# Five unread TensorE products in chunk 0's joins, and chunk 1's queries loaded ahead of weight piece 2

## The chip, the cores and the metric

The kernel runs on one core of one Trainium2 chip. The metric is the device time of one execution in microseconds (us). A profiled execution gives the trace, in which TensorE is PE, VectorE is DVE, ScalarE is ACT, GpSimd is POOL, and SyncE (SP) issues most of the DMA transfers.

## The reference

The kernel computes a DeltaNet attention block and then a SiLU feed-forward block on its output. Cut to what matters:

```python
# q, k, v: (4, 8, 768, 48); beta: (4, 8, 768)
k_n = k / (norm(k) + 1e-06)
state = zeros((B, H, D, D))
for t in range(S):
    y[:, :, t] = q[:, :, t] @ state
    v_old = k_n[:, :, t] @ state
    state += beta * outer(k_n[:, :, t], v[:, :, t] - v_old)
# bridge: (B, H, S, D) -> (B * S, H * D), 3072 tokens of 384
h = x @ w_in            # 384 x 2048
g = h * sigmoid(h)
return (g @ w_out)      # 2048 x 384
```

The weights arrive in 64-bit floating point, and the kernel turns them into 32 bits itself.

## The kernel before

The 768 steps of a sequence are cut into six chunks of 128, and a chunk into two halves of 64. Inside a chunk the recurrence is solved in matrix form: for each head a triangular matrix of 64 x 64 is inverted, and its blocks are put together on TensorE. Chunk 0 does this in its own way. `invert_first` inverts blocks of 16 x 16 on VectorE in 16 steps, and `joins` puts them together in ten stages for one half of the chunk: `corner`, `turned`, `straight` and `merge_half`, for the two groups of heads g = 0 and 1 in turn. Each stage is 32 or 64 small products on TensorE followed by copies out of PSUM by ScalarE and VectorE. The second merges (the last two stages) give the joined blocks `xi`. Then `solve(0)` starts: `inner` (tile pz, L859), whose results are copied out into `sums_of_w` (a slab) and `z`, then `first_outputs` (L905), which read the slab.

`joins(hf, between)` takes a list of things to do, one after each stage. `kept` is `busy(1)`: one product of 128 x 384 with the identity, into a PSUM bank of the CC pool, that nothing reads. `filled(n)` runs `fill` n times, `begin_next` starts the next piece of weights that has been asked for, `sized` scales chunk 0's values and does `begin_next`, and `none` does nothing. Ahead of `joins`, the 17 steps of the inverse have a list of words of their own; "n" there is one `busy(1)` too.

The weights are loaded in 16 pieces, `w_in` first. `fetch_w_in(i)` issues three transfers of 256 KB. `narrow` turns a piece into 32 bits in steps: two on ScalarE (L231, L232) when the piece is begun, one on VectorE (L236), and one on VectorE (L240) with an addition on GpSimd (L244) to end it. `fill` takes the steps in the order of the pieces.

Transfers go out on SyncE's queue in the order of the program, each tied to the one before. The list `pace` makes the next transfer wait for a given instruction, and `deep` makes each transfer wait until the one two places ahead of it has landed:

```python
        if pace or depth:
            behind(dma, pace.pop() if pace else line[-2], Sync)
```

`load_q(1)` issues the six transfers of chunk 1's queries into the room of `sums_of_g`; TensorE transposes them (L521) between the two halves of chunk 0's first outputs.

All instructions are pinned in the written order on their engines: `pin` ties each to the one before it on the same engine. After `joins(0, ...)` a text of one-letter words sets the order of the rest of the first stretch: "s" is a step of `solve`, "f" a `fill`, "T" and "q" transposes of chunk 1's keys and queries, "j" products of the second half's joins, "r" a step of the feed-forward block, "b" is `begin_next`.

Of the kernel before, what the change touches and what calls it, by code (L numbers as in the profile page):

```python
# [19 lines left out]
def kernel(  # L20
# [11 lines left out]
    B, H, S, D = q.shape  # L32
# [8 lines left out]
    T = 32  # L41
# [36 lines left out]
    pins = {}  # L78

    def pin(op):  # L80

        engine = op.ins.engine
        if engine in pins:
            behind(op, pins[engine])
        pins[engine] = op
        return op

    line, pace, depth = [], [], []
# [21 lines left out]
    def together(*parts):  # L110
        for _ in zip_longest(*parts):
            pass
# [58 lines left out]
    def linked(fetch, *args, of=None):  # L171

        pace.append(of or line[-1])
        fetch(*args)

    def deep(fetch, *args):

        depth.append(True)
        fetch(*args)
        depth.pop()  # L180
# [22 lines left out]
    seen_on = pin(nc.vector.memset(seen[:], 0.0)).ins.engine  # L203
# [9 lines left out]
    for e in range(2):  # L213
        for g in range(2):
            to, of = slice(HH * e + HH // 2 * g, HH * e + HH // 2 * (g + 1)), slice(HH // 2 * g, HH // 2 * (g + 1))
# [129 lines left out]
    def busy(n=1, after=None, how=NoSync):  # L345

        for _ in range(n):
            pw = bank(CC, "pw")
            done = pin(nc.tensor.matmul(  # L349
                pw[:, 0:DM], lhsT=ident[:],  # L350
                rhs=states[0][:].rearrange("p u a w -> p (u a w)")[:, 0:DM], start=True, stop=True,
            ))
            if after is not None:
                behind(done, after, how)
                after = None
# [158 lines left out]
    def turn(c, b, j, room, by_vector=False):  # L514

        if j == 0:
            kq_room(c, b)
        src, kq = (kbufs[c % 2], queries[c] if c < 2 else None)[j][:, b], kqs[c, b]
        pt = bank(room, "pt")
        for p in range(NP):  # L520
            pin(nc.tensor.transpose(  # L521
                pt[:, p * C : (p + 1) * C], src[:, p].rearrange("p e w -> p (e w)"), ident[:]
            ))
        ptv = pt[:].rearrange("p (a t) -> p a t", a=NP)
        if j == 1:
            if by_vector:
                pin(nc.vector.tensor_scalar(
                    out=kq[:, :, j, :], in0=ptv, scalar1=-1.0, scalar2=None, op0=ALU.mult
                ))
            else:  # L530
                pin(nc.scalar.mul(kq[:, :, j, :], ptv, -1.0))
        elif by_vector:
            pin(nc.vector.tensor_copy(out=kq[:, :, j, :], in_=ptv))
        else:
            pin(nc.scalar.copy(kq[:, :, j, :], ptv))

    def score(c, b, js, rooms, evacuate):

        g, u = b // HB, b % HB
        if (c, g) not in aps:  # L540
            aps[c, g] = {}
        for j in js:
            if j not in aps[c, g]:
                aps[c, g][j] = work.tile([P, HB, H, W], FP32, name=f"ap{j}", tag=f"ap{j}", bufs=2)
        ap, kq, n = aps[c, g], kqs[c, b], len(js)
        pa = [bank(room, f"pa{e}") for e, room in enumerate(rooms)]
        for p in range(NP):
            for e, hf in ((0, 0), (1, 1), (0, 1), (1, 0)):
                rows, half = slice(W * e, W * e + D), slice(W * hf, W * (hf + 1))
                pin(nc.tensor.matmul(  # L550
                    pa[e][half, p * n * W : (p + 1) * n * W], lhsT=kq[rows, p, 0, half],
                    rhs=kq[rows, p, js[0] : js[-1] + 1, half], start=True, stop=True,
                ))
        for e in range(2):
            of = pa[e][:, 0 : NP * n * W].rearrange("p (a j t) -> p a j t", a=NP, j=n)
            for i, j in enumerate(js):
                evacuate(j, e, ap[j][:, u, e::2, :], of[:, :, i, :])
# [6 lines left out]
    def by_act(to, of):  # L564
        return pin(nc.scalar.copy(to, of))  # L565
# [246 lines left out]
    def merge_half(g, hf, second):  # L812

        y = ys[0][:, g]
        pms = [bank(room, "px" if second else "py") for room in (A, CC)]
        for i in range(HH // 2):
            for e in range(2):
                n, k = 2 * i + e, hf ^ e ^ g
                even, odd = slice(W * k, W * k + T), slice(W * k + T, W * (k + 1))
                if second:  # L820
                    to, left, right = even, y[odd, n, :], xis[g][odd, n, T:W]
                else:
                    left = aps[0, g][0][even, n // H, n % H, T:W]
                    to, right = odd, xes[0][even, g * HH + n, :]
                yield pin(nc.tensor.matmul(
                    pms[k][to, T * i : T * (i + 1)], lhsT=left, rhs=right, start=True, stop=True
                ))
        for k, by in enumerate((by_act, by_dve)):
            e, half = hf ^ k ^ g, slice(W * k, W * k + T) if second else slice(W * k + T, W * (k + 1))
            of = pms[k][half, 0 : HH // 2 * T].rearrange("p (h t) -> p h t", t=T)  # L830
            by(xis[g][half, e::2, T:W] if second else y[half, e::2, :], of)
# [411 lines left out]
    class Piece:  # L1243
# [3 lines left out]
        def begin(self):  # L1247
            if self.steps is None:
                kind, i = self.name
                self.steps = (narrow_w_in if kind == "in" else narrow_w_out)(i)  # L1250
                next(self.steps)
# [73 lines left out]
    def first_score(b):  # L1325

        def evacuate(j, e, to, of):
            by_act(to, of)

        score(0, b, (0,), (A, CC), evacuate)  # L1330
# [49 lines left out]
    for n in range(1 + Q):  # L1380
        done = next(inv)
        for word in [
            "s2", "n s3", "u0", "u1 w0", "w1", "u2", "u3", "w2", "w3", "n", "N", "", "", "", "", "", "",
        ][n].split():
            at = int(word[1:] or 0)
            if word[0] == "b":
                busy(1, done, Sync)
            elif word[0] == "n":
                busy(1)
            elif word[0] == "s":  # L1390
                first_score(at)
            elif word[0] == "u":
                turn(0, at, 1, M)
            elif word[0] == "w":
                score(0, at, (1,), (A, CC), lambda j, e, to, of: by_act(to, of))
            else:
                begin(("in", 0))
# [6 lines left out]
    def joins(hf, between=()):  # L1404

        for stage in (
            corner(0, hf), corner(1, hf), turned(0, hf), turned(1, hf), straight(0, hf), merge_half(0, hf, False),
            straight(1, hf), merge_half(1, hf, False), merge_half(0, hf, True), merge_half(1, hf, True),
        ):
            yield from stage  # L1410
            for what in between[:1]:
                for one in what if isinstance(what, tuple) else (what,):
                    one()
            between = between[1:]
# [4 lines left out]
    def filled(n):  # L1419
        return lambda: fill(n)  # L1420

    def fetched():
        linked(fetch_w_in, 2, of=pins[seen_on])
        deep(load_q, 1)
        for i in (3, 4, 5, 6):
            deep(fetch_w_in, i)

    def sized():
# [3 lines left out]
    def none():  # L1432
        pass

    together(joins(0, [none, fetched, none, sized, filled(2), none, filled(1), none, begin_next, none]))

    pieces = chained(hidden(0, 0), hidden(0, 1), project())

# [132 lines left out]
                pieces = chained(feed_forward(1, 0), feed_forward(1, 1))  # L1571

    for text in (
        "s f s f T f q T s q T j5 j4 j8 j8 f j5 f q r T j20 j5 j8 j4 j16 j5 j4 b r q r f j4 j4 f W7 r b j4 f2 j4 j4 j32 r f e j6 j6 b j8 j4 f j4 j20 f j4 r j4 j99 l h f2 b l s w2 f r2 l p r s l w3 r p r l p f l2 f l3 b l f l2 s l f l p l3 r l3 s l f l r l2 p f s2 l2 H f l4 f r2 f p2 v l g G r i p i p r2 f i i2 r i r i b l i r f r i r b r2 i b b b i2 r2 i2 f b i5 r6 f r f r i2 r2 f r i r f r f i4 f i b r2 i3 b f b f r i r i f k r f r z i b r s r2 t z s b r2 b s m2 r5 t f t m f t m2 r s t m r b s b m r m2 s r m r m r c m2 s m r m t b m2 s m2 b m f m2 t r t m3 r m s m",
    ):
        script(text)
    for c in range(1, NCH):
# [59 lines left out]
```

## Time and profile before

| | |
|---|---|
| median of 3 runs | 641.72 us (639.18 to 643.24) |
| profiled execution | 639.7 us |
| its span, first to last instruction | 638.0 us |
| mean granted TensorE clock | 0.986 |
| TensorE busy | 621.5 us, 97% of the span |
| VectorE, ScalarE, GpSimd busy | 399.1, 216.7, 94.2 us |

The span is cut into 40 slices on the page, and a digit gives the busy share of a slice in tenths; the row PEclk gives the TensorE clock that was granted. Busy times of TensorE hold pipelined products, so that a busy TensorE can still run at half its clock. Times of instructions are given from the span's start.

### The profile page before, as it was taken

The page shows a single profiled execution, that of the slowest core. Times are in us where ns is not written, and L with a number is a line of the kernel's source. Part 1 is how long each engine was busy: PE and PEld are TensorE (multiplying, and loading weights), DVE is VectorE, ACT ScalarE, POOL GpSimd, SP SyncE. Part 2 cuts the span into 40 slices and gives each one's busy share as a digit, 9 for nine tenths or more (in the row PEclk, how much of TensorE's full clock was granted, in tenths as well). Part 3 has the DMA queues.
Part 4 walks back from the last instruction along what each step waited for, and adds up shares of the span by engine and source line. Part 5 has one row for each costly group of instructions (what it writes and reads, how often), then busy time and mean ns, then how long its engine had stood idle before and what let it go on. Part 6 is the DMA issues. An engine that isn't in the chain of part 4 may idle for free.

```text
span 638.0 us, 21886 instructions
## 1 busy us (share of the span) xinstructions
PE 621.5 (97%) x9650; PEld 547.8 (86%) x9650; DVE 399.1 (63%) x902; ACT 216.7 (34%) x510; POOL 94.2 (15%) x95
## 2 busy tenths in 40 slices
PE   8789999999999999999999999999999999999997
PEld 5678788666789989989989989989999989989997
DVE  6855879998765975654976564986564964212112
ACT  3565665152251122451122451122451122441110
POOL 5423531246010020020020010020001000000000
PEclk9968999999999999999999999999999999999999
DMA  7845554160459242369242259233173033100101
GB/s 152 182 124 179 179 128 100 52 149 3 102 120 163 57 89 24 83 126 147 39 107 29 69 122 160 56 88 37 43 142 72 19 83 34 39 15 1 26 0 26
DMA packets 141694, 53.68 MB, mean 84 GB/s; under 512 B 113296, under 2 KB 135056, under 8 KB 141600
## 3 DMA queue, kind: packets, MB, share of 16 engines
q1 hardware_dynamic: 141120, 51.62, 39.6%
q8 instruction: 76, 1.25, 0.9%
q10 hardware_dynamic: 480, 0.67, 0.3%
q14 instruction: 18, 0.15, 0.1%
HBM read 39.62 MB, written 10.49 MB: 79 GB/s over the span
## 4 chain that ended last, share of the span: by engine, by line
PE 95%; DVE 3%; issue 1%; POOL 0%; ACT 0%; DVEq 0%; POOLq 0%
PE phid L1068 40%; PE px L1175 17%; PE py L1175 13%; PE po L1103 7%; PE pa L550 3%; PE pz L859 2%; PE ph L847 2%; PE pyc L940 2%; PE pyc L927 2%; PE pu L879 2%; PE pt L521 1%; PE px L801 1%; PE py L801 1%; PE pw L349 1%; PE pl L752 1%
## 5 line engine op out<-in xcount | busy, mean ns | idle before, releaser
L1068 PE MATMUL phid<-xT,w_in 128*128 128x256 f32 x1152 | 258.7, 383 | 0.1
L1068 PEld LDWEIGHTS phid<-xT,w_in 128*128 128x128 f32 x1152 | 217.1, 191 | 30.6 <-issue 1.0
L1078 ACT ACTIVATE gT<-phid 128x512 f32<-128x512 f32 x88 | 52.6, 598 | 145.0 <-PE phid L1068 140.7
L648 DVE SCALAR_TENSOR_TENSOR rank<-g,step,x 128x31 f32<-128x31 f32 (+15 forms) x124 | 49.7, 401 | 35.8 <-DMA g<-blocks 32.4
L1157 DVE TENSOR_TENSOR sums_of_g<-gT 128x384 f32<-128x384 f32 (+1 forms) x60 | 29.7, 514 | 56.5 <-ACT gT L1078 45.9
L1175 PE MATMUL py<-w_out,sums_of_g 128*128 128x192 f32 x320 | 56.8, 329 | 0.0
L1175 PE MATMUL px<-sums_of_w,sums_of_g 128*128 128x192 f32 x320 | 56.6, 329 | 0.0
L1175 PEld LDWEIGHTS px<-sums_of_w,sums_of_g 128*128 128x128 f32 x320 | 52.2, 190 | 0.5
L1175 PEld LDWEIGHTS py<-w_out,sums_of_g 128*128 128x128 f32 x320 | 52.2, 190 | 0.4
L653 DVE TENSOR_TENSOR x<-x,rank 128x31 f32<-128x31 f32 (+15 forms) x124 | 42.5, 343 | 4.3
L488 POOL TENSOR_TENSOR vf<-vf,n_slot 128x768 f32<-128x768 f32 x10 | 15.2, 1538 | 168.4 <-DMA vf<-in_v_dram 168.4
L886 DVE TENSOR_TENSOR state<-state,pu 48x384 f32<-48x384 f32 x44 | 24.3, 552 | 23.2 <-PE pu L879 22.3
L565 ACT COPY xT<-pyc 48x128 f32<-48x128 f32 (+2 forms) x120 | 31.2, 260 | 1.6
L509 DVE STREAM_TRANSPOSE kq<-stage 128x512 f32<-128x512 f32 x28 | 28.3, 1114 | 3.6 <-DMA stage<-in_q_dram 3.5
L1175 PE MATMUL py<-w_out,gT 128*128 128x192 f32 x160 | 28.4, 329 | 0.0
L1175 PE MATMUL px<-sums_of_w,gT 128*128 128x192 f32 x160 | 28.4, 329 | 0.0
L1175 PE MATMUL px<-w_out,gT 128*128 128x192 f32 x160 | 28.0, 327 | 0.0
L859 PEld LDWEIGHTS pz<-vf,xi 64*64 64x64 f32 x768 | 25.1, 142 | 3.2 <-issue 2.2
L571 POOL COPY g<-x 64x256 f32<-64x256 f32 x4 | 5.0, 1247 | 152.3 <-DVE x L656 152.3
L1175 PEld LDWEIGHTS px<-w_out,gT 128*128 128x128 f32 x160 | 26.4, 190 | 0.5
L859 PE MATMUL pz<-vf,xi 64*64 64x48 f32 x768 | 26.8, 226 | 0.0
L1175 PEld LDWEIGHTS py<-w_out,gT 128*128 128x128 f32 x160 | 26.1, 190 | 0.3
(202 smaller groups left out, 827.7 us busy)
## 6 DMA issues: line engine op xcount, KB each, us to landing
vf<-in_v_dram SPq DMA_DIRECT2D x48, 96.0 KB, 2.7
out_dram<-o SPq DMA_DIRECT2D x42, 96.0 KB, 2.2
w_out<-in_moe_w_in_dram SPq DMA_DIRECT2D x12, 256.0 KB, 3.3
sums_of_w<-in_moe_w_out_dram SPq DMA_DIRECT2D x8, 384.0 KB, 3.7
blocks<-ap SPq DMA_DIRECT2D x40, 64.0 KB, 1.9
kb<-in_k_dram SPq DMA_DIRECT2D x12, 192.0 KB, 4.4
kb<-in_k_dram SPq DMA_DIRECT2D x24, 96.0 KB, 4.6
raw<-in_moe_w_in_dram SPq DMA_DIRECT2D x9, 256.0 KB, 3.5
```

The lines of the kernel that those rows point to most:

```text
L509: pin(nc.vector.transpose(out=kqs[c, b][:, :, j, :].rearrange("p a (i m) -> p a m i", i=T), in_=src.rearrange("p a (m d) -> p a m d", d=D) ...
L550: pin(nc.tensor.matmul(pa[e][half, p * n * W : (p + 1) * n * W], lhsT=kq[rows, p, 0, half], rhs=kq[rows, p, js[0] : js[-1] + 1, half], sta ...
L565: return pin(nc.scalar.copy(to, of))
L648: pin(nc.vector.scalar_tensor_tensor(out=tv, in0=g[:, 0:m, m : m + 1].to_broadcast([P, m, n]), scalar=step[:, m : m + 1], in1=x[:, m : m + ...
L653: yield pin(nc.vector.tensor_tensor(out=x[:, 0:m, m:T], in0=x[:, 0:m, m:T], in1=tv, op=ALU.add))
L859: yield pin(nc.tensor.matmul(pz[rows, n * D : (n + 1) * D], lhsT=xis[g][rows, u * H + 2 * p + e, :], rhs=vfs[c][rows, hf, g * HB + u, p, : ...
L886: pin(nc.vector.tensor_tensor(out=to, in0=to, in1=by_heads(pu[of]), op=ALU.add))
L1068: pin(nc.tensor.matmul(ph[:, j * GT : (j + 1) * GT], lhsT=w_in[:, a, (2 * f + j) * P : (2 * f + j + 1) * P], rhs=xTs[c, hf][:, a, :], star ...
L1078: pin(nc.scalar.activation(out=hidden_of(c, hf, f), in_=ph[:], func=ACTF.Silu, scale=-0.5 if in_blocks(c) else 0.5))
L1103: pin(nc.tensor.matmul(pos[i][:, 0:DM], lhsT=hidden_of(0, hf, f // 2)[:, at : at + C], rhs=w_outs[f // HFF][:, f % HFF, :], start=(f == 0) ...
L1157: pin(nc.vector.tensor_tensor(out=sums_of_g[:, k, fs], in0=of[0], in1=of[1], op=op))
L1175: pin(nc.tensor.matmul(to, lhsT=at, rhs=quarter(f, *b) if isinstance(b, tuple) else sums_of_w[b][:, f], start=start and f == 0, stop=f == ...
```

## The change

One more "n" stands in the words of the inverse's steps. In the list of `joins(0, ...)` four of the entries become `kept`, one of them beside `fetched`. The filling step that ended piece 0 moves from the seventh place to the tenth, and `begin_next`, which begins piece 2, moves from the ninth place out of the list to the head of the text as the word "b". In `fetched` the queries of chunk 1 go ahead of weight piece 2: they now wait for VectorE's instruction, and piece 2 is issued `deep`, as pieces 3 to 6 are.

```diff
-            "s2", "n s3", "u0", "u1 w0", "w1", "u2", "u3", "w2", "w3", "n", "N", "", "", "", "", "", "",
+            "s2", "n s3", "u0", "u1 w0", "w1", "u2", "u3", "w2", "w3", "n", "N", "", "n", "", "", "", "",
...
     def fetched():
-        linked(fetch_w_in, 2, of=pins[seen_on])
+        pace.append(pins[seen_on])
         deep(load_q, 1)
-        for i in (3, 4, 5, 6):
+        for i in (2, 3, 4, 5, 6):
             deep(fetch_w_in, i)
...
-    together(joins(0, [none, fetched, none, sized, filled(2), none, filled(1), none, begin_next, none]))
+    together(joins(0, [none, (fetched, kept), kept, sized, filled(2), kept, none, none, kept, filled(1)]))
...
-        "s f s f T f q T s q T j5 j4 j8 j8 f j5 f q r T ...
+        "b s f s f T f q T s q T j5 j4 j8 j8 f j5 f q r T ...
```

More of the change, by code (lines that the diff above doesn't have):

```diff
@@ L1573 @@
     for text in (
-        "s f s f T f q T s q T j5 j4 j8 j8 f j5 f q r T j20 j5 j8 j4 j16 j5 j4 b r q r f j4 j4 f W7 r b j4 f2 j4 j4 j32 r f e j6 j6 b j8 j4 f j4 j20 f j4 r j4 j99 l h f2 b l s w2 f r2 l p r s l w3 r p r l p f l2 f l3 b l f l2 s l f l p l3 r l3 s l f l r l2 p f s2 l2 H f l4 f r2 f p2 v l g G r i p i p r2 f i i2 r i r i b l i r f r i r b r2 i b b b i2 r2 i2 f b i5 r6 f r f r i2 r2 f r i r f r f i4 f i b r2 i3 b f b f r i r i f k r f r z i b r s r2 t z s b r2 b s m2 r5 t f t m f t m2 r s t m r b s b m r m2 s r m r m r c m2 s m r m t b m2 s m2 b m f m2 t r t m3 r m s m",
+        "b s f s f T f q T s q T j5 j4 j8 j8 f j5 f q r T j20 j5 j8 j4 j16 j5 j4 b r q r f j4 j4 f W7 r b j4 f2 j4 j4 j32 r f e j6 j6 b j8 j4 f j4 j20 f j4 r j4 j99 l h f2 b l s w2 f r2 l p r s l w3 r p r l p f l2 f l3 b l f l2 s l f l p l3 r l3 s l f l r l2 p f s2 l2 H f l4 f r2 f p2 v l g G r i p i p r2 f i i2 r i r i b l i r f r i r b r2 i b b b i2 r2 i2 f b i5 r6 f r f r i2 r2 f r i r f r f i4 f i b r2 i3 b f b f r i r i f k r f r z i b r s r2 t z s b r2 b s m2 r5 t f t m f t m2 r s t m r b s b m r m2 s r m r m r c m2 s m r m t b m2 s m2 b m f m2 t r t m3 r m s m",
     ):
```

## The prediction

> **What bounds the kernel now.** I read the page first, then stretches of the span, the chain that ended last, and the rows of ScalarE and of SyncE's queue around the edit.
>
> ```profile
> PE 621.5 (97%) x9650; PEld 547.8 (86%) x9650; DVE 399.1 (63%) x902; ACT 216.7 (34%) x510; POOL 94.2 (15%) x95
> PE   8789999999999999999999999999999999999997
> PEclk9968999999999999999999999999999999999999
> ```
>
> TensorE is the bound: past the first tenth of the span it hardly pauses, so a delay of its work near 43 us is carried to the end unless a later pause takes it up. The same rows place the weak spot: slices 1 to 4 of the clock row (16 us each) read 9, 9, 6, 8. Stretches of the span show it closer; after the PE, weight-load, DVE, ACT and POOL columns comes the granted clock.
>
> ```profile
> 24.00:29.90 5.90, 3.88 (x178) 2.96 (x168) 5.32 (x9) 2.94 (x7) 5.87 (x5) 1.00 0.79 195
> 29.90:43.50 13.60, 10.38 (x373) 9.91 (x373) 6.31 (x14) 7.28 (x15) 4.82 (x4) 0.50 0.52 131
> 43.50:53.80 10.30, 9.95 (x307) 8.90 (x302) 7.58 (x12) 6.23 (x13) 1.85 (x1) 1.00 0.48 150
> 53.80:57.20 3.40, 3.40 (x12) 2.76 (x11) 0.25 (x1) 2.13 (x4) 1.83 (x1) 0.50 0.52 177
> ```
>
> Chunk 0's joins run at half clock from 29.9 to 43.5 us, and 3.4 us of the first hidden layer do so again from 53.8. In the first two rows TensorE idles 2.0 and 3.2 us. The chain of work that ended last, in order of time, says what those stretches hold.
>
> ```profile
> 36.79 0.96 DVE w_in L240
> ...
> 39.67 3.47 PE pz L859 x62
> ...
> 43.25 0.90 PE py L905 x42
> ...
> 53.31 2.38 PE phid L1068 x6
> 55.69 0.85 PE pt L521 x4
> 56.55 1.67 PE phid L1068 x6
> ...
> 58.68 1.49 PE phid L1068 x6
> ...
> 64.27 1.12 issue
> ```
>
> A narrowing step of weight piece 0 (L240 on VectorE) stands on the chain; then come the first inner products (pz) at half clock, then the first outputs (L905). The first outputs read what ScalarE copies out of pz, so ScalarE's queue is what this edit has to be read against. Its rows, with start and duration:
>
> ```profile
> 37.58 0.88 ACT L231 ACTIVATE w_in<-w_out 128x768 f32<-128x768 f32 x1
> 38.37 0.97 ACT L232 ACTIVATE w_out<-w_out,plus 128x768 int32<-128x768 uint32 x1
> 39.70 0.36 ACT L565 COPY xi<-px 32x256 f32<-32x256 f32 x1 [0.37 <-PE px L825]
> 41.64 0.48 ACT L565 COPY sums_of_w<-pz 128x384 f32<-128x384 f32 x1 [1.58 <-PE pz L859]
> ...
> 52.94 0.91 ACT L231 ACTIVATE w_in<-w_out 128x768 f32<-128x768 f32 x1
> ...
> 80.60 0.93 ACT L231 ACTIVATE w_out<-w_out 128x768 f32<-128x768 f32 x1
> 81.41 1.01 ACT L232 ACTIVATE w_out<-w_out,plus 128x768 int32<-128x768 uint32 x1
> 82.30 0.48 ACT L565 COPY z<-pz 128x384 f32<-128x384 f32 x1
> ```
>
> The first two rows are the opening steps of weight piece 2, ahead of the last merge copy (39.70) and of the pz copy (41.64). They wait for nothing, because the piece is there.
>
> **The change: the loads.** Before, SyncE issues piece 2's three transfers from 29.22 us and then the six of chunk 1's queries. After, the queries take piece 2's place behind the same VectorE instruction, and piece 2 follows, each transfer held until the one two places ahead of it has landed. SyncE's rows show how slowly that chain walks; the two landing rows are those of piece 1's load and of the queries.
>
> ```profile
> 29.22 0.81 SPq L291 DMA_DIRECT2D w_out<-in_moe_w_in_dram  x2
> ...
> 33.37 0.38 SPq L142 DMA_DIRECT2D sums_of_g<-in_q_dram  x1
> 33.98 0.61 SPq L142 DMA_DIRECT2D sums_of_g<-in_q_dram  x1
> ...
> 42.62 0.35 SPq L291 DMA_DIRECT2D w_out<-in_moe_w_in_dram  x1
> 43.82 0.35 SPq L291 DMA_DIRECT2D w_out<-in_moe_w_in_dram  x1
> ...
> 48.64 0.33 SPq L291 DMA_DIRECT2D w_out<-in_moe_w_in_dram  x1
> ```
> ```profile
> L291 SPq DMA_DIRECT2D raw<-in_moe_w_in_dram x3: 430/437/619, 26.3 to 27.4; - x3
> DMA to landing us min/median/max: 4.4/4.4/4.4
> ```
> ```profile
> L142 SPq DMA_DIRECT2D sums_of_g<-in_q_dram x6: 378/602/1439, 33.4 to 40.4; - x6
> DMA to landing us min/median/max: 3.0/3.1/3.2
> ```
>
> In the profile of before, six queries and then three weight transfers also stand in this chain, only the weights are piece 3. From the first query's issue (33.37) to the landing of the piece's third transfer (48.64, where the transfer two places on is let go) it took 15.3 us; from the second query's issue (33.98) 14.7 us. After, the first query goes at 29.2, so piece 2 is whole at 44.5 at the earliest. The second query must wait for piece 1's last transfer, which lands at 27.4 + 4.4 = 31.8; from there 14.7 us give 46.5. I take 45.6, between the two, as both strands must end. Before, ScalarE began on piece 2 at 37.58.
>
> **The change: what waits behind it.** In the new program order ScalarE does both last merge copies, then L231 and L232 of piece 2, and only then the copy out of pz. The wait for piece 2 therefore stands ahead of that copy. Behind it on ScalarE are the pz copies, the first xT copy and the copies of chunk 1's transposes; VectorE's own copy of pz waits for ScalarE's, as it does now:
>
> ```profile
> DVE z L568 <- ACT sums_of_w L565: 2.1, 1, 2.1
> ```
>
> TensorE's next instructions are the first outputs, and nothing in its order can go ahead of them. From L231's start to that of the copy behind it the trace has 82.30 - 80.60 = 1.70 us, and the copy takes 0.48. So the first outputs start at 45.6 + 1.7 + 0.5 + 0.1 = 47.9, against about 43.1 now: **4.8 us late**, with 3.7 and 5.7 as the bounds from the landing.
>
> **The change: the clock.** TensorE then idles from the end of pz (40 to 43.2) to 47.9, five to eight microseconds. The stretch ahead of the present fall at 29.9 had TensorE busy two thirds of the time and still lost the clock, so an empty one does. The first outputs and the transposes restart at half clock. The half-clock stretches here are 13.6 and 3.4 us, so 3.4 or a multiple; the restart falls anywhere in one, and must fill enough of it. I take 2.9 us at half clock, that is 1.45 us lost, between 0 and 3.4; 0.2 of it is lost now too (43.1 to 43.5). By 1.3 us the end moves. By the Trainium skill, "TensorE: Matmul & The Clock Gate", section "What's actually happening", one busy window of about 3.4 us opens the clock again, which would make this 1.7 lost and the sum 0.25 us more; no row here shows a restart after a pause of this length.
>
> The present stretch from 53.8 costs 2.38 + 1.67 - 2 x 1.49 = 1.1 us. Whether it comes back depends on where the windows fall in a shifted schedule: half, a gain of 0.5.
>
> **The change: the five products.** The nearest rows are the unread products at the start, cold and warm (two rows of records to a product):
>
> ```profile
> 2.40 3.96 PE pw L349 x6
> ...
> 11.07 0.84 PE pw L349 x2
> ...
> 74.40 1.08 PE ph L847 x64
> ```
>
> One costs 0.84 us at full and 1.32 at half clock, five 4.2 to 6.6. Against the 5.2 us that TensorE idles from 24.0 to 43.5, that is between a hold of 1.4 us and none; a gain if they hold the clock, since pz could then take near 1.1 us (64 products of a like shape, 74.40) in place of 3.5. Either way pz ends between about 40 and 44.7, before the copy out of it can start at 47.3. I cost them at **nothing**; ScalarE's wait covers them. Were that cover gone, they would cost up to 1.4 us or save up to about 2.4. The step that finishes piece 0 moves behind the merges too: L240 leaves the chain (0.96 us), and its GpSimd add goes with it.
>
> ```profile
> 37.89 1.85 POOL L244 TENSOR_TENSOR w_in<-w_in,raw 128x768 int32<-128x768 int32 x1 [4.38 <-DVE w_in L240]
> ```
>
> Both then run while ScalarE waits, near 40 to 43, and the hidden layer that reads them starts after 48: nothing.
>
> **The change: later pieces.** Piece 3 lands at 48.6 now and about 3 us later after; ScalarE begins it at 52.94 now and 4.8 us later after. It keeps over 4 us of slack, and pieces 4 to 7 move with it. With TensorE later against the loads, its pause of 1.12 us at 64.27, in which it waits for nothing that the profile shows, may shrink; I count a third, 0.4.
>
> **The sum.** The profiled execution took 639.7 us (span 638.0 and 1.7 around it). 639.7 + 4.8 + 1.3 - 0.5 - 0.4 = 644.9. The median of the runs shown, 641.7, stands 2.0 above that execution. If some of these 2.0 us come from joins that run slower, ScalarE's wait swallows them after the change, for it counts from SyncE's chain; I carry half, 1.0. The forecast is **645.9 us**, 0.65% above the median; its own range is 642.5 to 648.7.
>
> **Rival 1: the clock makes it dearer.** The restart needs two windows instead of one (3.4 us lost, 3.2 more than now), the stretch of 53.8 returns, no later pause shrinks, and piece 2 lands at its late bound: 639.7 + 5.7 + 3.2 + 1.0 = 649.6. For it: 29.9 to 43.5 is four windows in a row at half clock although TensorE was busy three quarters of them. Against it: the first outputs and transposes now keep the clock from 43.5 on. It decides if the clock reads half beyond 52 us.
>
> **Rival 2: not slower, because the chain of loads walks faster.** Piece 3's quickest transfer landed 2.7 us after its issue:
>
> ```profile
> DMA to landing us min/median/max: 2.7/3.0/3.3
> ```
>
> If four steps in a row (two queries behind the second one's, the sixth among them, and a weight transfer) took 2.7 us each from 31.8, piece 2 would be whole at 42.6, the first outputs at 44.9, 1.8 late; the pause then stays under one stretch of 3.4 us, the clock need not fall, and with 0.5 and 0.4 off and 0.2 of half clock spared the time is 640.4 us, under the median. It decides at a landing of 43 us. The queries' rows, 3.0 to 3.2, and the chain's own 15.3 us speak against it. [...]
>
> **Rival 3: it does what it says.** Piece 2 is there when ScalarE reaches it, about 40.5, and the products hold the clock through the joins: pz saves 2.4, L240 leaves the chain for 1.0, the stretch of 53.8 goes for 1.1, against one product in the way for 0.8. 639.7 - 2.4 - 1.0 - 1.1 + 0.8 = 636.0. It needs the chain of loads in 11.3 us where it took 15.3.
>
> **How the numbers follow.** Forecast 0.48, rival 1 0.38, rival 2 0.09, rival 3 0.05. One per cent, 6.4 us, is about what a measurement of this kernel can tell from no change: 635.3 to 648.1 is within it. Slower by more are most of rival 1 (0.35) and the top fifth of the forecast (0.10), 0.45; faster by more is less than half of rival 3, 0.02; within, 0.53. The range takes in the forecast and rival 1 up to 650.5 and ends at 641.0 below, which leaves out rivals 2 and 3 and the rare dearer end.
>
> **What would show it.** Right: L231 of piece 2 starts near 45.6 with a wait for its load, behind both merge copies; TensorE is empty from the end of pz to about 48; the clock is at half there; queries issued from 29.2. The second products of pz would show the joins' clock, whichever it is, without effect. Wrong: L231 starts before 43, or the first outputs before 45.5, or the pauses later in the span shrink by as much as the stall.

## The result and the profile after

| kernel | median us | range | ratio to before, 95% interval |
|---|---|---|---|
| before, beside it | 641.29 | 639.18 to 643.57, 6 runs | |
| after | 648.62 | 646.37 to 649.87, 6 runs | 1.0107 [1.0075, 1.0139] |

The change makes the kernel slower by 1.07%, about 7 us. The profiled execution took 649.04 us with a span of 647.3.

ScalarE's rows around the second merges of the kernel after, to be held against those of before:

```profile
44.78 0.36 ACT L565 COPY xi<-px 32x256 f32<-32x256 f32 x1 [2.25 <-PE px L825]
47.03 0.90 ACT L231 ACTIVATE w_in<-w_out 128x768 f32<-128x768 f32 x1 [1.89 <-DMA w_out<-in_moe_w_in_dram]
47.84 0.96 ACT L232 ACTIVATE w_out<-w_out,plus 128x768 int32<-128x768 uint32 x1
48.69 0.46 ACT L565 COPY sums_of_w<-pz 128x384 f32<-128x384 f32 x1
```

L231 of piece 2 waits for its load until 47.03, and the copy out of pz stands behind it. TensorE's rows at the same place:

```profile
42.06 1.65 PE L349 MATMUL pw<-state,ident 128*128 128x384 f32 x2
43.64 1.06 PE L825 MATMUL px<-xi,xe_y 32*32 32x32 f32 x32
44.64 3.65 PE L859 MATMUL pz<-vf,xi 64*64 64x48 f32 x64
49.21 1.56 PE L905 MATMUL py<-ap,sums_of_w 64*64 64x64 f32 x48 [0.92 <-ACT sums_of_w L565]
```

The first outputs start at 49.21, 6.3 us later than before, but TensorE stands empty for only 0.92 of it: pz itself starts 5 us later, at 44.64, at half clock, with an unread product of 1.65 us just ahead of the last merge. SyncE's rows show that the chain of loads kept the pace that was expected, from a later start:

```profile
31.83 0.38 SPq L142 DMA_DIRECT2D sums_of_g<-in_q_dram  x1
...
41.31 0.35 SPq L291 DMA_DIRECT2D w_out<-in_moe_w_in_dram  x1
...
46.94 0.33 SPq L291 DMA_DIRECT2D w_out<-in_moe_w_in_dram  x1
```

From the first query to the last landing of piece 2 it is 46.94 - 31.83 = 15.1 us (15.3 had been read off piece 3). The first query went 2.6 us later because VectorE's instruction that releases it stands behind the first products of the joins, which started late. Stretches of the span, with the granted clock behind the five engines:

```profile
18.90:25.70 6.80, 6.80 (x123) 5.04 (x114) 6.08 (x22) 3.13 (x8) 0.75 (x2) 0.50 0.79 141
25.70:35.90 10.20, 9.02 (x294) 6.62 (x296) 4.44 (x8) 4.97 (x11) 6.30 (x5) 1.00 0.56 137
35.90:53.00 17.10, 15.73 (x377) 12.97 (x367) 8.12 (x16) 8.92 (x18) 3.31 (x2) 0.50 0.53 143
53.00:83.70 30.70, 28.36 (x738) 23.61 (x737) 19.24 (x35) 19.21 (x34) 15.06 (x12) 1.00 0.55 173
83.70:87.10 3.40, 3.40 (x39) 2.41 (x38) 3.16 (x13) 1.24 (x3) 0.23 (x1) 0.50 0.01 1
```

The half clock from 18.9 to 25.7 lies ahead of the first new product, so it is not the change's; the execution profiled before had none there, and part of the 9.3 us between the two profiles is that. The last unread product that both kernels share starts at 24.12 in before (first row) and at 28.08 in after (second row, which holds the first new product too):

```profile
24.12 0.91 PE L349 MATMUL pw<-state,ident 128*128 128x384 f32 x2
```
```profile
28.08 1.56 PE L349 MATMUL pw<-state,ident 128*128 128x384 f32 x4
```

So 4.0 of the 5 us by which pz is late were there before TensorE reached the change. The chain that ended last holds something new, later pauses of TensorE:

```profile
79.75 0.95 PE ph L847 x55
80.70 1.60 issue
```
```profile
93.92 0.86 PE pu L879 x64
94.79 0.90 PE pyc L940 x63
95.68 1.76 issue
97.45 0.21 PE pyc L940
97.66 2.35 PE phid L1068 x10
```

Both fall inside a burst of short products (in the second, one product before its end), and nothing that the profile shows is waited for. The same place of before runs through:

```profile
85.93 0.87 PE pu L879 x64
86.80 0.90 PE pyc L940 x64
87.69 2.81 PE phid L1068 x12
```

### The profile page after: what moved, and what is told of

Read it like the earlier page. It is cut to its first block, busy times and chain, and to the rows that moved or that the text cites. A ratio compares the mean times of both kernels' runs of the same rounds, so it can differ in the third digit from the quotient of the medians.

```text
span 647.3 us, 21907 instructions
## 1 busy us (share of the span) xinstructions
PE 631.5 (98%) x9660; PEld 553.3 (85%) x9660; DVE 398.0 (61%) x902; ACT 216.8 (33%) x510; POOL 93.5 (14%) x95
## 3 DMA queue, kind: packets, MB, share of 16 engines
q8 instruction: 76, 1.25, 0.9%
## 4 chain that ended last, share of the span: by engine, by line
PE 91%; DMA 5%; ACT 1%; issue 1%; DVE 0%; POOL 0%; SPq 0%; POOLq 0%
PE phid L1068 38%; PE px L1175 16%; PE py L1175 12%; PE po L1103 7%; PE pa L550 4%; DMA w_out<-in_moe_w_in_dram 3%; PE pz L859 2%; PE ph L847 2%; PE pyc L940 2%; PE pyc L927 2%; PE pu L879 2%; DMA sums_of_g<-in_q_dram 1%; PE pw L349 1%; PE px L801 1%; PE py L801 1%
## 5 line engine op out<-in xcount | busy, mean ns | idle before, releaser
L488 POOL TENSOR_TENSOR vf<-vf,n_slot 128x768 f32<-128x768 f32 x10 | 14.9, 1506 | 167.7 <-DVE sums_of_g L1157 50.4
```

## The experiments

Two theories stood against each other: ScalarE's wait ahead of the pz copy makes the loss (theory 1, the prediction), or the five products do (theory 2). Every ratio is against runs of the kernel before on the same chip.

**The products alone (e1).** Loads and narrowing steps stay as before.

```diff
-"n", "N", "", "", "", ...
+"n", "N", "", "n", "", ...
-joins(0, [none, fetched, none, sized, filled(2), none, filled(1), none, begin_next, none])
+joins(0, [none, (fetched, kept), kept, sized, filled(2), kept, filled(1), none, (begin_next, kept), none])
```

> The kernel before plus the five products alone; loads and narrowing steps as before. Theory 1 (ScalarE's wait for piece 2 ahead of the pz copy makes the loss, the products hide in TensorE's idle time): 640 to 642.5 us, no difference from before; L231 of piece 2 near 38 without a wait. Theory 2 (the products stand in TensorE's order at half clock, 1.3 us each, and shift where the 256-instruction fetches fall): 645 to 648 us, pz starts 3 to 5 us later than 39.7, and pauses without a visible releaser near 80 and 95 us.

Measured: 646.17 against 643.02 us, ratio 1.0057 [1.0030, 1.0084]. Theory 1 alone is refuted: the products cost about 3.7 us, and L231 of piece 2 starts at 42.13 without a wait. pz starts at 44.39, 4.8 us later than in before. One of the two pauses named is there, 1.43 us at 91.4.

**The load order and the moved steps without products (e2).**

```diff
-"n", "N", "", "n", "", ...
+"n", "N", "", "", "", ...
-joins(0, [none, (fetched, kept), kept, sized, filled(2), kept, none, none, kept, filled(1)])
+joins(0, [none, fetched, none, sized, filled(2), none, none, none, none, filled(1)])
```

> The change without its five products: queries ahead of piece 2, narrowing steps moved. Theory 1: 645 to 648 us, L231 of piece 2 waits for its load until 45 to 47, TensorE idle 4 us ahead of the first outputs. Theory 2: 641 to 643 us, the wait is hidden or small.

Measured: 646.68 us, ratio 1.0062 [1.0033, 1.0091]. TensorE's and ScalarE's rows show the wait that had been predicted. It is longer than in after, since pz starts 1.5 us earlier and piece 2 lands 2.9 us later, behind the 45 to 47 that had been expected:

```profile
43.12 3.65 PE L859 MATMUL pz<-vf,xi 64*64 64x48 f32 x64
52.10 1.56 PE L905 MATMUL py<-ap,sums_of_w 64*64 64x64 f32 x48 [5.33 <-ACT sums_of_w L565]
```
```profile
49.94 0.89 ACT L231 ACTIVATE w_in<-w_out 128x768 f32<-128x768 f32 x1 [6.35 <-DMA w_out<-in_moe_w_in_dram]
```

ScalarE waits 6.35 us for piece 2, TensorE 5.33 us for ScalarE. When TensorE goes on, the clock is at half for 4.0 us more:

```profile
46.80:52.10 5.30, 0.00 (x0) 0.00 (x0) 0.02 (x1) 2.11 (x3) 0.00 (x0) 0.50 0.54 180
52.10:56.10 4.00, 4.00 (x60) 3.79 (x60) 2.83 (x5) 2.05 (x4) 0.00 (x0) 0.50 0.48 152
```

**The change with piece 2 ahead of the queries again (e3).**

```diff
-        pace.append(pins[seen_on])
+        linked(fetch_w_in, 2, of=pins[seen_on])
         deep(load_q, 1)
-        for i in (2, 3, 4, 5, 6):
+        for i in (3, 4, 5, 6):
```

> The change with piece 2 loaded ahead of the queries again, as before; products and moved narrowing steps stay. Theory 1: 640 to 642 us, or a little under before. Theory 2: 645 to 648 us, as with the products alone.

Measured: 646.16 us, ratio 1.0051 [1.0024, 1.0079]. Without the wait the products' cost is left, as in e1.

**The change with piece 2 begun later (e4).**

```diff
-"b s f s f T f q T s q T j5 j4 ...
+"s f s f T f q T s q T b j5 j4 ...
```

> The change with the word b moved behind the second query transpose, so that L231 of piece 2 stands behind the pz copies and the first outputs' copies on ScalarE; loads, products and the rest as in the change. Theory 1: 640 to 643 us, the first outputs start when pz ends. Theory 2: 646 to 648.5 us, since the joins end late by themselves; only the 0.9 us between pz and the first outputs is saved.

Measured: 647.12 us, ratio 1.0052 [1.0019, 1.0085]. In microseconds this lies in theory 2's range, but the kernel before stood at 643.02 beside it. Against the change the ratio is 0.55% lower, 3.5 us or half of the loss, where theory 1 had all of it and theory 2 only 0.9 us. The first outputs start when pz ends, and the products' cost stays. In this profile the clock came back at 37.6, inside the joins, and the second row shows pz at full clock:

```profile
30.80:37.60 6.80, 5.88 (x134) 3.75 (x134) 2.71 (x6) 2.80 (x6) 2.62 (x2) 0.50 0.47 95
```
```profile
41.30 2.01 PE L859 MATMUL pz<-vf,xi 64*64 64x48 f32 x62
```

So the loss has two parts of about the same size, 0.57% by the products alone (e1) and 0.62% by the order alone (e2), against 1.07% for both, and each is gone without its own cause. The intervals reach about 0.3% to either side. The next runs ask what of the products costs, and whether the load order costs apart from the wait.

**The products 16 columns wide (e5).** As e1, with the same count of instructions and less of the time.

```diff
-                pw[:, 0:DM], ... rhs=...[:, 0:DM]
+                pw[:, 0:width], ... rhs=...[:, 0:width]      # 16 for the five, DM elsewhere
```

> The kernel before with the five products of the change, but 16 columns wide instead of 384: the same number of TensorE instructions in the same places, nearly none of their time. The products alone at full width measured 1.0057. If their cost is time in TensorE's order: ratio 0.999 to 1.002. If it is the shift of the 256-instruction fetches against the dense bursts: 1.004 to 1.007, with pauses at the same instruction counts (near 3490 and 4510) as with the full products.

Measured: 643.42 against 641.21 us, ratio 1.0036 [1.0014, 1.0058], between the two expectations. Its pause at the place of the burst L940, in the waits of TensorE from 84 to 100 us, and three rows of TensorE:

```profile
PE pyc L940 <- issue: 1.7, 1, 1.7
```
```profile
27.81 0.40 PE L349 MATMUL pw<-state,ident 128*128 128x16 f32 x2
37.82 0.61 PE L349 MATMUL pw<-state,ident 128*128 128x16 f32 x2
43.01 3.54 PE L859 MATMUL pz<-vf,xi 64*64 64x48 f32 x62
```

The narrow products are not free: one takes 0.40 us at full and 0.61 us at half clock, where a full one takes 0.91 and 1.65. By the rows of e5 and e1 the five take about 2.4 us in place of 5.8. They cost 0.36% in place of 0.57%, with overlapping intervals, so the run does not separate their time from their count. pz starts at 43.01, 3.4 us later than in before.

**The narrowing steps moved, nothing else (e6).**

```diff
-joins(0, [none, fetched, none, sized, filled(2), none, filled(1), none, begin_next, none])
+joins(0, [none, fetched, none, sized, filled(2), none, none, none, none, filled(1)])
-"s f s f T ...
+"b s f s f T ...
```

> The kernel before with only the narrowing steps moved (end of piece 0 and start of piece 2 behind the second merges); loads as before, no products. Theory (L240 leaves the chain, piece 2 is there in time): 0.9975 to 1.0005. Rival (ScalarE's two steps of piece 2 now stand ahead of the pz copy and hold it): 1.001 to 1.003.

Measured: 639.92 against 641.21 us, ratio 0.9982 [0.9963, 1.0002]: within the first expectation, but the interval reaches 1. L231 of piece 2 stands ahead of the pz copy here too and starts at 41.00 without a wait, so its place alone costs nothing; e2 differs from this run by the order of the loads alone.

**The load order with the late start, no products (e7), and again (e12).** As e4, with the list of e2 and without the "n".

> The change without its products and with the word b moved behind the second query transpose: queries ahead of piece 2, but ScalarE's wait for piece 2 no longer stands ahead of the pz copy. If the load order costs only through that wait: 0.997 to 1.002, against 1.0062 with the wait. If the later pieces or the busier queues cost as well: 1.004 to 1.007.

> Queries ahead of piece 2, no products, late start of piece 2, a second time on another chip. If it beats the kernel before: 0.995 to 0.9995 again. If the first measurement was luck of the clock's windows: 0.9995 to 1.003.

Measured: 639.52 against 641.21 us, 0.9973 [0.9952, 0.9994]; the second time 640.75 against 640.65, 1.0004 [0.9982, 1.0027]. On the mean, 0.999, it is not shown to beat the kernel before. It does show that the load order itself costs nothing: e2 differs by the place of the word "b" alone and stands at 1.0062, 0.7% or 4.7 us higher. TensorE's rows of e7 at that place have no pause between pz and the first outputs:

```profile
40.53 3.54 PE L859 MATMUL pz<-vf,xi 64*64 64x48 f32 x62
43.78 0.37 PE L905 MATMUL py<-ap,sums_of_w 64*64 64x64 f32 x2
```

**Both pieces begun behind the joins (e8).** A try at a faster version: loads as before, no products.

```diff
     def sized():
         size_half(0, pins[seen_on])
-        begin_next()
...
-joins(0, [none, fetched, none, sized, filled(2), none, filled(1), none, begin_next, none])
+joins(0, [none, fetched, none, sized, filled(2), none, none, none, none, filled(1)])
...
-"s f s f T f q T s q T j5 j4 ...
+"b s f s f T f q T s q T b j5 j4 ...
```

> A version meant to beat both: loads as before, no products, end of piece 0 behind the second merges, and ScalarE's two steps of piece 1 behind the merges too, those of piece 2 behind the second query transpose, so that no narrowing step of ScalarE stands inside the joins. If the copies that wait behind those steps (1.8 us near 32) are on the chain: 0.995 to 0.998. If TensorE's own pauses there set the pace: 0.999 to 1.001.

Measured: 640.28 against 641.21 us, 0.9990 [0.9970, 1.0011]. ScalarE's steps inside the joins were not what set their pace.

**Six and three narrow products behind the joins (e9, e10).** The first joins stay untouched, and only the count of TensorE's instructions ahead of the later bursts grows.

```diff
-... f j4 r j4 j99 l h f2 ...
+... f j4 r j4 j99 x6 l h f2 ...       # x3 in e10; x: busy(n), 16 columns
```

> The kernel before with six unread products of 16 columns behind the second half's joins (near 68 us): chunk 0's first joins untouched, 24 TensorE instructions more ahead of the bursts near 87 us. If the shift of the instruction fetches is what the narrow products cost: a pause of 1.2 to 2.5 us without a visible releaser at the end of the products L940 near 88 us (record 4510), which the kernel before does not have, and a ratio of 1.001 to 1.004. If the cost of the narrow products lay in the joins (waits, banks): no such pause, 0.999 to 1.001.

> The same with three narrow products, 12 instructions: the end of L940's burst stays 8 records short of the fetch that the six reach, so four long products behind it cover part of the fetch. Fetch theory: no pause at the end of L940 or one under 0.8 us, a ratio of 0.999 to 1.002. Joins theory: the same as with six.

Measured: 641.72 (e9) and 642.48 (e10) against 640.55 us, 1.0014 [0.9986, 1.0042] and 1.0042 [1.0012, 1.0072]. The chains of e9 and of e10 have the pause:

```profile
88.06 0.90 PE pyc L940 x62
88.96 0.76 issue
89.71 0.31 PE pyc L940 x2
```
```profile
84.63 0.90 PE pyc L940 x64
85.53 1.06 PE phid L1068 x4
86.59 1.02 issue
87.61 1.99 PE phid L1068 x8
```

Six products (24 instructions) put it two products ahead of the burst's end, three (12 instructions) four long products behind it: it sits at the same count of instructions, and moves against the work. That much of the theory is borne out. The sizes are not: 0.76 us where 1.2 to 2.5 had been expected, and three products measured dearer than six and than the 0.999 to 1.002 expected of them, with intervals that overlap.

**Narrow products beside the late start (e11).** e4 with its five products 16 columns wide; against e12 only they are added.

> The change with the late start of piece 2 and its five products 16 columns wide: against the run beside it only the narrow products are added. If 20 more TensorE instructions cost by themselves in this surrounding too: 0.3 to 0.5% above the run beside it, 1.0005 to 1.003 of before, with a pause at the end of the products L940 near 90 us. If they cost only beside the loads of before: the same as the run beside it, 0.995 to 1.000.

Measured: 642.76 against 640.65 us, 1.0040 [1.0014, 1.0066], 0.36% over the run beside it (e12), as e5 over before; by the two intervals that is between 0.0 and 0.7%. Against before it lies above both ranges, since e12 came out at 1.0004. pz starts at 42.17, against 39.39 in e12. Its chain has the pause too:

```profile
88.36 0.90 PE pyc L940 x63
89.25 2.10 issue
```

## Why the prediction was right, and where it was not

**The stall.** Right in kind and place, and near in size. The forecast had the first outputs 4.8 us late and 1.3 us lost to the half clock, 6.1 together; without the products (e2) TensorE waited 5.33 us and then ran 4.0 us at half clock, and e2 against e7 and e12 is 4.7 us of time. In the change itself less of the stall shows, 0.92 us in its profile and 0.55%, 3.5 us, between after and e4, since the joins end later.

**The loads.** The 15.3 us of the chain came out at 15.1 in after. In e2 it took 18.7 (31.14 to 49.85), as the second query waited 2.8 us for piece 1's load; from the second query it took 15.5, where 14.7 had been forecast. That they count from 29.2 was wrong: the start follows the joins' own start, 31.83 in this execution, and so piece 2 was whole at 46.94 and not at 45.6.

**The products, costed at nothing.** This step failed. "ScalarE's wait covers them" needed pz to end between 40 and 44.7; it ended at 48.3, in part for the clock's early stretch. And with the wait away (e1, e3, e4) they cost 0.5 to 0.6%, more than 3 us, where up to 1.4 had been reckoned without the cover. That reckoning let their time fill the 5.2 us in which TensorE idles. The waits of TensorE in before from 28 to 44 us show what 2.4 us of that idling are:

```profile
PE pl L765 <- issue: 1.6, 1, 1.6
...
PE pl L752 <- issue: 0.8, 1, 0.8
```

In these TensorE waits for no other engine, but for its next instructions, as the following paragraph shows. That a further product cannot fill such a pause, since it is an instruction too, is an argument and not measured. The joins did get longer. From the last shared product to pz it is 14.0 to 16.1 us in the eight kernels without products in the joins, and 15.8 to 18.4 in the six with them (18.0 in e5 and 16.6 in e11, with the narrow ones). The means, 14.9 and 16.9, are 2.0 us apart, with one profile of each kernel.

**What the pauses are.** The page of both kernels gives these transfers of instructions:

```profile
q8 instruction: 76, 1.25, 0.9%
```

1.25 MB in 76 transfers is 16.4 KB each. The kept traces have the start and the length of every one of them, and TensorE's records in order. In the 14 traces TensorE pauses 70 times for over 0.5 us without anything that it waits for. Counted in TensorE's records from the start, the places of all 70 are multiples of 256 apart, and each pause ends 1.2 to 1.9 us after one of the transfers has ended. So they are waits for the next 256 instructions. The pause at the burst L940 stands behind 4545 records. In the six kernels with the five products in the joins, wide or narrow, that is in the last product of the burst, and the pause is of 1.4 to 2.5 us; in before, e2, e6, e7, e8 and e12 it is among the long products behind the burst, and there is none. Twenty instructions more (two loads and two products in the records of each) shift that burst onto the boundary. The Trainium skill, "Runtime: NRT & Kernel Launch", section "Instruction fetch mechanics", says that an engine's instructions come in blocks of 16 KiB or 256 and that crossing a block is mostly hidden. The trace agrees with both: in after, 6 such pauses stand against 76 transfers. The crossing is not hidden in after where TensorE runs 256 short records in about 1.8 us (the rows of pu and pyc above).

How the products' cost divides is open. The longer joins (2.0 us) and the later pauses (those from 55 to 105 us sum to 2.6 to 4.4 us in the six kernels with the products, and to 0 to 1.9 in before, e2, e6, e7, e8 and e12) are each as large as the 2.3 us of the narrow products. e10, which leaves the first joins alone, cost as much as e5 with 1.0 us of pause.

**The later pauses.** The pause at 64.27 went away, as a third had been counted on, and those at 80.7 and 95.7 came: in after the term of -0.4 has the wrong sign. The half clock of 53.8 did not come back, as half had been counted on; the pause of 1.60 us at 80.7 lies ahead of another stretch, from 83.7.

**The rivals.** Rival 1's price, 649.6, is near the measured 648.6, and by its own sign, half clock beyond 52 us, it was met. But its mechanism is not there: the clock needed 4 us after the restart (to 53.0 in after, to 56.1 in e2) and not two stretches, and it reads half beyond 52 because the restart came late. Rival 2 needed piece 2 by 43 and had it at 46.9. Of rival 3 the products' part came true now and then (e3 and e4 had the clock back inside the joins), and saved less than the products cost.

**The sum.** The forecast rise was 4.2 us and the measured one is 7.3. Without the products (e2) it is 0.62%, 4.0 us; by the two ratios the products add 2.9. That e2 comes so near the 4.2 is partly luck: the stall and the clock cost 4.7 us in place of 6.1, and the 1.9 us taken off (0.5 and 0.4 for later stretches, and the 1.0 by which the median stood higher and that was not carried) were too much by about as much. That 648.6 still lies inside the forecast's own 642.5 to 648.7 is luck too, for that width was meant for the landing and the clock, and held nothing for the products.

## What to carry to other kernels

A step that is moved ahead on an in-order engine brings its wait with it: find when its data lands under the new order of loads, and what stands behind it; here one word moved by a few places was worth 4.7 us. Instructions that only fill an idle engine are not free even where the engine idles. Each takes its turn in the engine's order, the idle time may itself be a wait for instructions, and every later burst shifts against the blocks in which instructions are fetched; count them, and look for pauses without a releaser behind them. Compare several executions before a difference of a few microseconds is put down to an edit, since the clock's stretches fall differently in each.

## What the runs showed of the hardware

A pause without a visible releaser sits at a fixed count of TensorE's instructions, not at a place in the work: all 70 of over 0.5 us in these traces stand multiples of 256 records apart. At one of these counts it is 1.4 to 2.5 us at the end of one burst with the products in the joins, and 0.76 and 1.02 where 24 and 12 instructions were added later. In after the clock fell to half for 3.4 us from 83.7, 1.4 us behind a pause of 1.60; that the pause did it is not shown, and behind the pause of 2.10 us in e11 there is no half clock. The clock's half stretches also begin at different times in different executions: after has one from 18.9, ahead of the first new product, and before has none there. Two profiles of the same code (e7 and e12) have pz at 40.53 and 39.39.
